# Tail additions and reciprocal products on GpSimd, q's rounding copy on VectorE, and the tail's tanh ahead of q's reads, in a fused attention and rational MLP

## The chip, the cores and the metric

The kernel runs on one core of one Trainium2 chip. The metric is the device time of one execution in microseconds; the median of three runs before is 698.41 us (698.06 to 699.09).

## What is computed

Attention with a capped score, then a two-layer MLP with a rational activation. The reference, cut to what matters:

```
scores = q @ k.T / sqrt(64)                  # 4 batches, 12 heads, 448 tokens, head size 64
scores = cap * tanh(scores / cap)            # cap = 30
attn = exp(scores - max);  attn = attn / (sum(attn) + 1e-9)
x = (attn @ v) laid out as (1792, 768)
h = x @ w_in                                 # 768 x 2048
g = (a0 + a1 h + a2 h^2 + a3 h^3) / (1 + |b0| |h| + |b1| h^2 + 1e-6)
out = g @ w_out                              # 2048 x 768
```

The weights arrive as 64-bit floats and are converted on the chip. Since cap is at most 40 the kernel takes its branch without the maximum ("bounded").

## The kernel before

**Attention.** Two heads make a pair; there are 24 pairs, p = 0 to 23. For a pair the 448 keys fall into three tiles of 128 (n = 0, 1, 2) and a tail of 64 (n = 3), in the order 0, 1, 3, 2 (`ORDER`). `scores` puts one tile's scores into one of three PSUM tiles `ps` of two banks (`slot` says which); `softmax` runs tanh there in place (L417) and `exp` writes the exponentials to SBUF (L437). A whole tile is 128 x 896 (two heads side by side); the tail is 128 x 448, with head 0 on partitions 0 to 63 and head 1 on 64 to 127. The tensor `es` of a pair collects the sum of the exponentials over the key tiles: one addition of 128 x 896 for n = 1 and one for n = 2 (L449), and for the tail two additions of 64 x 448 (L446), all on VectorE.

`pv` multiplies by v on TensorE (L494) and VectorE copies the unnormalised output to `U` (L503). After every second pair `norm` adds `es` up over the partitions on TensorE ("sums", L519, into the PSUM bank `mi`), copies the result out (L523), moves it by four small DMAs to 32 partitions, takes reciprocals (L532, L533), writes them to `dn` in HBM and reads them back broadcast over partitions (`bc`). These DMAs are on GpSimd's queue, for the last norm on SyncE's. `xout` then multiplies U by `bc` (L552, VectorE).

`prep_qk(p + 2)` is called while pair p is worked on: TensorE transposes k into bank `mi` (L335, L337) and q into the unused second bank of the tail's `ps` tile (L341). VectorE rounds k to fp32r and takes the rest (L349, L350); ScalarE scales and rounds q (L355) and VectorE takes its rest (L358). These reads of q are called before the tail's tanh.

**Conversions and splits.** During pairs 5 to 8 four weight tiles are converted (`make_w`: ScalarE L688, VectorE L690, L693, L696, then L718 and L720). x is split into a high and a low part for each of six 128-row blocks and each half of the batches: `split_x`, L563 on ScalarE and L565 on VectorE for the first half; for the second half L563 and L569 on ScalarE and a DMA on GpSimd's queue that accumulates into the low part (L570).

**MLP.** 32 units (group g of two hidden blocks, half m, block y): `stage1` (L740), `rational` (L767 to L780), `stage2` (L805). The first units of half m = 1 need the second half's splits, and so the last norms.

**Order of the work.** Every operation is recorded with an assumed cost and its reads and writes; `Plan.flush` places them by a list scheduler (priority = place in the program less `early`), for the whole program at once, and emits each engine's stream in that order. On the chip each engine, and GpSimd's queue with its DMAs, runs its stream strictly in order. So another engine, cost or write key for one operation moves other operations too.

Of the kernel before, what the change touches and what calls it, by code (L numbers as in the profile page):

```python
# [235 lines left out]
class Body:  # L236
# [83 lines left out]
    def prep_qk(self, p):  # L320
# [18 lines left out]
        def tq():  # L339
            for c in range(4):  # L340
# [6 lines left out]
        self.busy(p, 0, [])  # L347
        self.op(PE, 440, tk, self.raw_keys(p, "rk"), bk + ["turn"], early=E_TR)
# [3 lines left out]
        self.op(PE, 400, tq, self.raw_keys(p, "rq"), bq + ["turn"], early=E_TR)  # L352
        self.busy(p, 1, bq)
        c1 = self.c["c1"]
        self.op(ACT, act_ns(448, True, 1), lambda: nc.scalar.activation(S[:, 2, 0:448], pq, AF.Identity, scale=c1),  # L355
                bq, [K("qh")], early=E_PR)
        self.op(DVE, dve_ns(448, 1),
                lambda: nc.vector.scalar_tensor_tensor(QL, pq, c1, f32(S[:, 2, 0:448]), ALU.mult, ALU.subtract),  # L358
                bq + [K("qh")], [K("ql")], early=E_PR)
# [49 lines left out]
    def softmax(self, p, n):  # L409
# [6 lines left out]
        if self.bounded:  # L416
            self.op(ACT, act_ns(448 * w, True), lambda: nc.scalar.activation(ps, ps, AF.Tanh),  # L417
                    ["table"], pk)
# [12 lines left out]
    def exp(self, p, n, src, sk, e, ek):  # L431
# [115 lines left out]
    def xout(self, p):  # L547
        k, x = divmod(p, 2)
        U = self.U[p]
        i = k % len(self.BC)  # L550
        bc = f32(self.BC[i])
        self.op(DVE, dve_ns(448), lambda: self.nc.vector.tensor_tensor(U, bc[:, x], U, ALU.mult),  # L552
                [("bc", i, x, j) for j in range(2)], [("u0", p), ("u1", p)])
# [18 lines left out]
    def attention(self):  # L572
# [17 lines left out]
        for p in range(P1):  # L590
            for m, n in enumerate(ORDER):
                self.scores(p, n)
                self.softmax(p, n)
                if (p, n) == (0, 0):
# [3 lines left out]
                if m == (2 if self.bounded else 3) and p + 2 < P1:  # L598
                    self.prep_qk(p + 2)
# [275 lines left out]
    def mlp(self, rest):  # L875
# [6 lines left out]
        for t in [t for t in rest if not self.last_norm(t // 2)]:  # L882
            self.xout(t)
# [15 lines left out]
        for u, (g, m, y) in enumerate(self.units):  # L899
# [5 lines left out]
            if u == 0:  # L905
                for t in rest:
                    self.xout(t)
# [301 lines left out]
```

## Time and profile before

| | us |
|---|---|
| median of 3 runs | 698.41 |
| the profiled execution, own time | 700.66 |
| its span, first to last instruction | 698.9 |
| busy: PE / DVE / ACT / POOL | 674.0 / 565.4 / 462.5 / 101.3 |

PE is TensorE's matmuls, PEld its weight loads, DVE is VectorE, ACT ScalarE, POOL GpSimd, SP SyncE. Issuing a DMA occupies a queue, and is not counted as the engine's arithmetic. A timeline row gives start, duration, engine, line, operation, output, inputs, how many instructions were merged, and in brackets the idle time before and what ended it. A matmul counts as busy from its start to a modelled end, so that a TensorE that is "busy" may still be slower than at its best.

### The profile page before, as it was taken

To read this page: it belongs to the slowest core of one execution; us is meant where nothing else is said; L and a number is where in the kernel's file an instruction comes from. 1 tells how busy PE (TensorE), PEld (TensorE's weight loads), DVE (VectorE), ACT (ScalarE), POOL (GpSimd) and SP (SyncE) were. 2 spreads that over 40 slices of the span, in tenths; PEclk is the share of its full clock that TensorE was granted. 3 is DMA by queue.
4 is the path that set the end of the run, shared out by engine and by line. 5 is a ranking of instruction groups with operands and counts; after the bars stand their busy time and mean duration, and the time that the engine had idled before them with its cause. 6 is when DMAs were issued, how large, how long until landed. Compare 5 with 4: busy or idle time off the path is not lost.

```text
span 698.9 us, 9641 instructions
## 1 busy us (share of the span) xinstructions
PE 674.0 (96%) x3685; PEld 546.2 (78%) x3685; DVE 565.4 (81%) x706; ACT 462.5 (66%) x575; POOL 101.3 (15%) x164
## 2 busy tenths in 40 slices
PE   7999889999999899999999999999999999999986
PEld 4554445444546799999999999999999999999986
DVE  4588999999884979866998698699779869878783
ACT  5699879899996887756557448546655744754520
POOL 4012223223232200011002001101100200110000
PEclk9799999999999999999999999999999999999999
DMA  6638665554315644167119417713922751692044
GB/s 146 144 87 198 156 148 130 129 131 118 84 36 120 122 143 163 45 123 159 58 45 160 90 45 156 139 46 78 174 50 85 139 109 46 131 210 67 23 181 163
DMA packets 81912, 79.95 MB, mean 114 GB/s; under 512 B 48960, under 2 KB 69184, under 8 KB 81856
## 3 DMA queue, kind: packets, MB, share of 16 engines
q1 hardware_dynamic: 70496, 53.74, 26.4%
q0 software_dynamic: 11360, 25.50, 21.3%
q8 instruction: 31, 0.51, 0.3%
q14 instruction: 25, 0.20, 0.1%
HBM read 50.73 MB, written 25.65 MB: 109 GB/s over the span
## 4 chain that ended last, share of the span: by engine, by line
PE 76%; DVE 12%; issue 4%; ACT 3%; SPq 2%; DMA 2%; POOL 0%; DVEq 0%; POOLq 0%
PE ps L740 32%; PE ps L805 16%; PE mi L805 8%; PE pv L805 8%; PE pv L494 5%; PE ps L405 4%; DVE arena_f L449 2%; DVE arena_f L446 2%; PE ps L316 1%; ACT ps L417 1%; DVE arena_r L358 1%; DMA arena_r<-dn 1%; DVE arena_r L349 1%; SPq L283 1%; PE ps L341 1%
## 5 line engine op out<-in xcount | busy, mean ns | idle before, releaser
L740 PE MATMUL ps<-arena_r,ring 128*128 128x512 f32 (+1 forms) x1152 | 249.5, 368 | 1.9 <-DMA arena_r<-arena_f 1.7
L740 PEld LDWEIGHTS ps<-arena_r,ring 128*128 128x128 f32 x1152 | 209.2, 188 | 28.4 <-DMA arena_r<-arena_f 2.1
L805 PE MATMUL ps<-arena_r,etiles 128*128 128x384 f32 x462 | 91.1, 338 | 0.0
L417 ACT ACTIVATE ps<-ps 128x896 f32<-128x896 f32 (+1 forms) x96 | 76.4, 815 | 16.0 <-PE ps L405 11.0
L283 POOL DMA_DIRECT2D sums<-arena_f x42 | 36.5, 868 | 341.6 <-ACT arena_f L837 337.5
L771 DVE SCALAR_TENSOR_TENSOR arena_f<-arena_f,bab 128x896 f32<-128x896 f32 x32 | 36.8, 1150 | 60.2 <-ACT arena_f L768 60.2
L767 ACT ACTIVATE arena_f<-ps,b 128x896 f32<-128x896 f32 x32 | 32.3, 1011 | 77.2 <-PE ps L740 77.2
L805 PEld LDWEIGHTS ps<-arena_r,etiles 128*128 128x128 f32 x462 | 81.8, 189 | 1.6 <-ACT etiles L779 0.3
L805 PE MATMUL pv<-arena_r,etiles 128*128 128x384 f32 x231 | 77.5, 337 | 0.0
L805 PE MATMUL mi<-arena_r,etiles 128*128 128x384 f32 x231 | 77.3, 336 | 0.0
L437 ACT ACTIVATE etiles<-ps,acap 128x896 f32<-128x896 f32 x72 | 72.5, 1014 | 0.6
L779 ACT CAST etiles<-arena_f 128x896 fp32r<-128x896 f32 x32 | 30.3, 946 | 61.6 <-DVE arena_f L778 61.5
L405 PEld LDWEIGHTS ps<-arena_r 64*128 64x128 f32 x432 | 37.9, 190 | 37.1 <-ACT arena_r L355 10.5
L494 PE MATMUL pv<-etiles,ring 128*64 128x448 f32 x264 | 60.4, 566 | 0.6 <-DVE arena_f L503 0.6
L405 PE MATMUL ps<-arena_r 64*128 64x448 f32 x432 | 59.0, 396 | 0.9 <-DVE arena_r L350 0.6
L776 DVE SCALAR_TENSOR_TENSOR arena_f<-arena_f,one 128x896 f32<-128x896 f32 x32 | 36.8, 1149 | 13.8 <-ACT arena_f L774 13.8
L805 PEld LDWEIGHTS pv<-arena_r,etiles 128*128 128x128 f32 x231 | 43.7, 189 | 1.2
L805 PEld LDWEIGHTS mi<-arena_r,etiles 128*128 128x128 f32 x231 | 43.7, 189 | 0.0
L805 PE MATMUL ps<-ring,etiles 128*128 128x384 f32 x210 | 42.2, 335 | 0.8 <-DVE arena_f L834 0.8
L688 ACT ACTIVATE arena_f<-arena_f 128x768 f32<-128x768 f32 x32 | 29.2, 911 | 17.5 <-DMA arena_f<-in_moe_w_in_dram 9.2
L805 PEld LDWEIGHTS ps<-ring,etiles 128*128 128x128 f32 x210 | 36.9, 188 | 1.6 <-DVE arena_f L834 1.1
L775 DVE SCALAR_TENSOR_TENSOR arena_f<-arena_f,a,ps 128x896 f32<-128x896 f32 x32 | 36.6, 1144 | 0.6
(113 smaller groups left out, 1096.3 us busy)
## 6 DMA issues: line engine op xcount, KB each, us to landing
sums<-arena_f POOLq DMA_DIRECT2D x42, 384.0 KB, 5.9
arena_f<-in_moe_w_out_dram SPq DMA_DIRECT2D x16, 768.0 KB, 4.1
arena_f<-in_moe_w_in_dram SPq DMA_DIRECT2D x16, 768.0 KB, 8.7
out_dram<-arena_f SPq DMA_DIRECT2D x13, 384.0 KB, 2.3
ring<-in_q_dram SPq DMA_DIRECT2D x44, 112.0 KB, 3.7
arena_r<-dn POOLq DMA_DIRECT2D x22, 224.0 KB, 4.0
ring<-in_k_dram SPq DMA_DIRECT2D x33, 128.0 KB, 2.9
ring<-in_v_dram SPq DMA_DIRECT2D x11, 384.0 KB, 4.7
```

The costliest lines, as they stand in the source:

```text
L283: self.op(eng, (625 if local else 450) if eng == SP else 1050, lambda: e.dma_start(out, in_, **accum), r, w, nbytes=nbytes, **kw)
L405: m = nc.tensor.matmul(self.PS[i][:, j, 0:448], st[r], mv[r], start=y == 0, stop=y == 2)
L417: self.op(ACT, act_ns(448 * w, True), lambda: nc.scalar.activation(ps, ps, AF.Tanh), ["table"], pk)
L437: self.op(ACT, act_ns(448 * w, sk[0][0] == "ps", 1), lambda: nc.scalar.activation(e, src, AF.Exp, scale=acap), sk + ["table"], [ek])
L494: m = nc.tensor.matmul(self.PV[64 * j:64 * j + 64, 0:448], st, mv, start=c == 0, stop=c == 3)
L740: r = nc.tensor.matmul(po[:, ts], w[:, y, kc], x, start=kc == 0 and z == 0, stop=kc == KC - 1 and z == 2)
L767: self.op(ACT, act_ns(n, True, 1), lambda: T.activation(Bt, h, AF.Abs, scale=b[:, 0:1]), hk, bk)
L771: self.op(DVE, dve_ns(n, 1), lambda: stt(Bt, C, bab[:, 1:2], Bt, ALU.mult, ALU.add), ck + ["bab"], bk)
L775: self.op(DVE, dve_ns(n, 1), lambda: stt(A, A, a[:, 1:2], h, ALU.add, ALU.mult), hk, ak)
L776: self.op(DVE, dve_ns(n, 1), lambda: stt(Bt, Bt, one, C, ALU.add, ALU.mult), ck, bk)
L779: self.op(ACT, act_ns(n, False), lambda: T.copy(GH(), A), ak, K("gh", ig) + first)
L805: r = nc.tensor.matmul(po[n][:, 0:384], st, mv[:, 384 * n:384 * n + 384], start=(y == 0 and x == 0), stop=(y == self.NCH - 1 and x == 2))
```

## The change

Four edits. The tail's two additions into `es` go from VectorE to GpSimd, behind the addition of tile n = 2. `xout` goes to GpSimd, except where it is called late (for pairs 21, 22 and 23, in `mlp`). q's scaling and rounding goes from ScalarE to VectorE. And `prep_qk` is called in two parts around the tail's `softmax`: the transposes before, the reads of k and q behind; the tail's tanh declares both banks of its PSUM tile as written, so that q's reads stand behind it.

```
+def pool_ns(n):
+    return 2.0 * n + 100
...
-    def prep_qk(self, p):
+    def prep_qk(self, p, part=None):
...
+        if part != 1:
+            self.busy(p, 0, [])
+            self.op(PE, 440, tk, self.raw_keys(p, "rk"), bk + ["turn"], early=E_TR)
+        if part is None:
+            self.convert_k(S, pk, bk, K)
+        if part != 1:
+            self.op(PE, 400, tq, self.raw_keys(p, "rq"), bq + ["turn"], early=E_TR)
+            self.busy(p, 1, bq)
+        if part == 1:
+            self.convert_k(S, pk, bk, K)
+        if part == 0:
+            return
+        qh = S[:, 2, 0:448]
+        self.op(DVE, dve_ns(448, 1), lambda: nc.vector.tensor_scalar(qh, pq, c1, None, ALU.mult),
+                bq, [K("qh")], early=E_PR)
...
-        self.op(ACT, act_ns(448, True, 1), lambda: nc.scalar.activation(S[:, 2, 0:448], pq, AF.Identity, scale=c1),
-                bq, [K("qh")], early=E_PR)
...
             self.op(ACT, act_ns(448 * w, True), lambda: nc.scalar.activation(ps, ps, AF.Tanh),
-                    ["table"], pk)
+                    ["table"], [("ps", i), ("psb", i)])
...
-        if n == 0:
+        if n in (0, 3):
             return
         es, ks = self.es[p % 3], [("es", p % 3)]
-        if n == 3:
-            for j in range(2):
-                r = slice(64 * j, 64 * j + 64)
-                self.op(DVE, dve_ns(448),
-                        lambda r=r, j=j: nc.vector.tensor_tensor(es[r, j], es[r, j], e[r, 0], ALU.add), [ek], ks)
-            return
         a, ak = self.etile(p, 0) if n == 1 else (es, None)
         self.op(DVE, dve_ns(896), lambda: nc.vector.tensor_tensor(es, a, e, ALU.add), [ek] + [ak] * (n == 1), ks)
+        t, tk = self.etile(p, 3)
+        for j in range(2 if n == 2 else 0):
+            r = slice(64 * j, 64 * j + 64)
+            self.op(POOL, pool_ns(448),
+                    lambda r=r, j=j: nc.gpsimd.tensor_tensor(es[r, j], es[r, j], t[r, 0], ALU.add), [tk], ks)
...
-    def xout(self, p):
+    def xout(self, p, late=False):
...
+        eng, e = (DVE, self.nc.vector) if late else (POOL, self.nc.gpsimd)
+        self.op(eng, dve_ns(448) if late else pool_ns(448), lambda: e.tensor_tensor(U, bc[:, x], U, ALU.mult),
...
                 self.scores(p, n)
+                if self.bounded and m == 2 and p + 2 < P1:
+                    self.prep_qk(p + 2, 0)
                 self.softmax(p, n)
+                if self.bounded and m == 2 and p + 2 < P1:
+                    self.prep_qk(p + 2, 1)
```

What the scheduler makes of it, at two places. In the rows below the lines of the changed kernel are its own: L464 are the tail additions, L568 `xout`, L459 the additions of tiles 1 and 2, L365 and L368 q's copy and rest, L373 and L374 k's, L518 the copy of U, L287 DMAs. The streams of a pair are alike from pair to pair but for the conversions.

**VectorE**, an odd pair in the middle of attention, where the reciprocals of a norm fall into it. Before:

```order
L449 TENSOR_TENSOR arena_f<-etiles 128x896
L503 COPY arena_f<-pv 128x448
L446 TENSOR_TENSOR arena_f<-arena_f 64x448
L532 TENSOR_SCALAR arena_f<-arena_f,guard 32x56
L533 RECIPROCAL arena_f<-arena_f 32x56
L446 TENSOR_TENSOR arena_f<-arena_f 64x448
L349 CAST arena_r<-mi 128x512
L449 TENSOR_TENSOR arena_f<-arena_f,etiles 128x896
L350 TENSOR_TENSOR arena_r<-mi,arena_r 128x512
L358 SCALAR_TENSOR_TENSOR arena_r<-ps_130,c_61,arena_r 128x448
```

Now, the same pair:

```order
L373 CAST arena_r<-mi 128x512
L374 TENSOR_TENSOR arena_r<-mi,arena_r 128x512
L459 TENSOR_TENSOR arena_f<-etiles 128x896
L365 TENSOR_SCALAR arena_r<-ps_130,c_61 128x448
L547 TENSOR_SCALAR arena_f<-arena_f,guard 32x56
L548 RECIPROCAL arena_f<-arena_f 32x56
L368 SCALAR_TENSOR_TENSOR arena_r<-ps_130,c_61,arena_r 128x448
L518 COPY arena_f<-pv 128x448
L459 TENSOR_TENSOR arena_f<-arena_f,etiles 128x896
```

The two tail additions are gone from the stream, q's copy has come in ahead of q's rest, and the addition of tile 2, on which GpSimd's additions wait, is followed by the next pair's reads of k.

**GpSimd's queue**, from the four small DMAs of the norm of pairs 20 and 21 to the accumulations of the second half's splits. Before:

```order
L283 DMA arena_f<-arena_f 8x1x56 x4
L283 DMA arena_r<-arena_f 128x2x448
L283 DMA dn<-arena_f 32x56
L283 DMA arena_r<-arena_f 128x2x448
L283 DMA arena_r<-dn 64x896 x2
L283 DMA arena_r<-arena_f 128x2x448 x4
```

Now:

```order
L464 TENSOR_TENSOR arena_f<-arena_f 64x448
L287 DMA arena_f<-arena_f 8x1x56
L287 DMA arena_r<-dn 64x896 x2
L464 TENSOR_TENSOR arena_f<-arena_f 64x448
L287 DMA arena_f<-arena_f 8x1x56 x3
L464 TENSOR_TENSOR arena_f<-arena_f 64x448
L568 TENSOR_TENSOR arena_f<-arena_r,arena_f 128x448 x2
L464 TENSOR_TENSOR arena_f<-arena_f 64x448
L287 DMA dn<-arena_f 32x56
L287 DMA arena_r<-arena_f 128x2x448 x2
L287 DMA arena_r<-dn 64x896 x2
L568 TENSOR_TENSOR arena_f<-arena_r,arena_f 128x448
L287 DMA arena_r<-arena_f 128x2x448 x4
```

The additions of pairs 22 and 23 and the products of pairs 18 and 19 now stand between the small DMAs and the reciprocals' way to HBM (`dn`); both first accumulations stand ahead of the broadcast (the second `arena_r<-dn`; the first is that of pairs 18 and 19), and the product of pair 20 behind it.

## Rows read from the trace of the kernel before

**Rows 1.** The page: busy tenths of PE, DVE, POOL in 40 slices.
```profile
PE   7999889999999899999999999999999999999986
...
DVE  4588999999884979866998698699779869878783
...
POOL 4012223223232200011002001101100200110000
```

**Rows 2.** Busy time by stretch: window, length, PE, PEld, DVE, ACT, POOL, clock, DMA.
```profile
63.45:101.55 38.10, 33.61 (x196) 16.32 (x196) 36.56 (x56) 31.47 (x41) 9.49 (x18) 0.96 0.71 172
109.60:167.42 57.82, 53.71 (x341) 27.52 (x340) 54.56 (x80) 52.99 (x70) 16.93 (x32) 1.00 0.55 129
167.42:205.43 38.01, 37.95 (x244) 18.93 (x242) 33.62 (x52) 35.29 (x46) 11.13 (x21) 1.00 0.26 69
```

**Rows 3.** Timeline of PE: the tail's scores of pairs 3, 4 and 5.
```profile
40.91 0.89 PE L316 MATMUL ps<-arena_r 128*128 128x448 f32 x3
...
48.07 0.88 PE L316 MATMUL ps<-arena_r 128*128 128x448 f32 x3
...
56.12 0.87 PE L316 MATMUL ps<-arena_r 128*128 128x448 f32 x3
```

**Rows 4.** What PE waited for, 60 to 170 us: total, times, longest.
```profile
PE mi L335 <- DVE arena_f L523: 3.5, 4, 1.7
PE ps L316 <- ACT etiles L437: 3.4, 3, 1.7
```

**Rows 5.** Groups of instructions, 0 to 330 us, shapes apart: busy us, mean ns.
```profile
L446 DVE TENSOR_TENSOR arena_f<-arena_f 64x448 f32<-64x448 f32 x48 | 29.6, 616 | 3.4 <-ACT arena_f L437 1.7
...
L449 DVE TENSOR_TENSOR arena_f<-arena_f,etiles 128x896 f32<-128x896 f32 x24 | 26.0, 1082 | 3.6 <-ACT etiles L437 3.0
...
L358 DVE SCALAR_TENSOR_TENSOR arena_r<-ps,c,arena_r 128x448 fp32r<-128x448 f32 x23 | 15.6, 679 | 3.5 <-ACT arena_r L355 2.0 <-ACT arena_f L437 1.2 <-ACT ps L417 0.3
...
L355 ACT ACTIVATE arena_r<-ps,c 128x448 fp32r<-128x448 f32 x23 | 14.8, 642 | 4.0 <-PE ps L341 3.9
...
L552 DVE TENSOR_TENSOR arena_f<-arena_r,arena_f 128x448 f32<-128x448 f32 x24 | 14.3, 616 | 8.4 <-DMA arena_r<-dn 8.4
```

**Rows 6.** Timeline of POOL at the start: its own instructions that are no DMA.
```profile
1.51 0.29 POOL masks.py:199 TENSOR_SCALAR_AFFINE_SELECT ident<-ident 128x128 f32<-128x128 f32 x1
...
4.55 1.08 POOL L186 MEMSET ring<- 128x256 f32 x4
```

**Rows 7.** Groups of DVE, 0 to 330 us: conversion and split instructions with two SBUF inputs.
```profile
L693 DVE SCALAR_TENSOR_TENSOR arena_f<-arena_f 128x768 int32<-128x768 int32 x11 | 10.5, 953 | 0.2
...
L565 DVE TENSOR_TENSOR arena_r<-arena_f,arena_r 128x896 fp32r<-128x896 f32 x6 | 6.5, 1082 | 0.9 <-ACT arena_r L563 0.9
```

**Rows 8.** Timeline of ACT, pair 15: q's rounding copy and the tail's tanh.
```profile
145.28 0.63 ACT L355 ACTIVATE arena_r<-ps,c 128x448 fp32r<-128x448 f32 x1 [0.22 <-PE ps L341]
...
147.16 0.53 ACT L417 ACTIVATE ps<-ps 128x448 f32<-128x448 f32 x1 [0.36 <-DVE arena_r L358]
```

**Rows 9.** Timeline: pair 21's last tile-2 addition, and the sums that need it.
```profile
199.09 1.02 DVE L449 TENSOR_TENSOR arena_f<-arena_f,etiles 128x896 f32<-128x896 f32 x1
...
203.12 0.96 PE L519 MATMUL mi<-arena_f 128*32 128x448 f32 x8
```

**Rows 10.** Timeline: the hand-over from attention to the MLP.
```profile
206.30 2.00 POOL L283 DMA_DIRECT2D arena_f<-arena_f  x4 [3.79 <-DVE arena_f L523]
...
213.46 1.09 DVE L449 TENSOR_TENSOR arena_f<-arena_f,etiles 128x896 f32<-128x896 f32 x1
...
213.79 0.87 POOL L283 DMA_DIRECT2D dn<-arena_f  x1
...
218.11 1.11 POOL L283 DMA_DIRECT2D arena_r<-dn  x2
...
224.93 0.62 DVE L552 TENSOR_TENSOR arena_f<-arena_r,arena_f 128x448 f32<-128x448 f32 x1 [6.80 <-DMA arena_r<-dn]
...
234.82 1.09 PE L740 MATMUL ps<-arena_r,ring 128*128 128x512 f32 x4 [1.70 <-DMA arena_r<-arena_f]
```

More of the change, by code (lines that the diff above doesn't have):

```diff
@@ L346, in prep_qk, with convert_k @@
         K = lambda s: (name, s)
-        self.busy(p, 0, [])
-        self.op(PE, 440, tk, self.raw_keys(p, "rk"), bk + ["turn"], early=E_TR)
+        c1 = self.c["c1"]
+        if part != 1:
[13 more added lines that the diff above has]
+                bq, [K("qh")], early=E_PR)
+        self.op(DVE, dve_ns(448, 1),
+                lambda: nc.vector.scalar_tensor_tensor(QL, pq, c1, f32(qh), ALU.mult, ALU.subtract),
+                bq + [K("qh")], [K("ql")], early=E_PR)
+    def convert_k(self, S, pk, bk, K):
+        nc = self.nc
         self.op(DVE, dve_ns(512), lambda: nc.vector.tensor_copy(S[:, 1, :], pk), bk, [K("kh")], early=E_PR)
@@ L351, in prep_qk @@
                 bk + [K("kh")], [K("kl")], early=E_PR)
-        self.op(PE, 400, tq, self.raw_keys(p, "rq"), bq + ["turn"], early=E_TR)
-        self.busy(p, 1, bq)
-        c1 = self.c["c1"]
-        self.op(ACT, act_ns(448, True, 1), lambda: nc.scalar.activation(S[:, 2, 0:448], pq, AF.Identity, scale=c1),
-                bq, [K("qh")], early=E_PR)
-        self.op(DVE, dve_ns(448, 1),
-                lambda: nc.vector.scalar_tensor_tensor(QL, pq, c1, f32(S[:, 2, 0:448]), ALU.mult, ALU.subtract),
-                bq + [K("qh")], [K("ql")], early=E_PR)
     def busy(self, p, n, r):
@@ L551, in xout @@
         bc = f32(self.BC[i])
-        self.op(DVE, dve_ns(448), lambda: self.nc.vector.tensor_tensor(U, bc[:, x], U, ALU.mult),
+        eng, e = (DVE, self.nc.vector) if late else (POOL, self.nc.gpsimd)
+        self.op(eng, dve_ns(448) if late else pool_ns(448), lambda: e.tensor_tensor(U, bc[:, x], U, ALU.mult),
                 [("bc", i, x, j) for j in range(2)], [("u0", p), ("u1", p)])
@@ L597, in attention @@
                     self.load_v(1, [(self.qset(1)[0], "ql")])
-                if m == (2 if self.bounded else 3) and p + 2 < P1:
+                if not self.bounded and m == 3 and p + 2 < P1:
                     self.prep_qk(p + 2)
@@ L882, in mlp @@
         for t in [t for t in rest if not self.last_norm(t // 2)]:
-            self.xout(t)
+            self.xout(t, True)
         rest = [t for t in rest if self.last_norm(t // 2)]
@@ L906, in mlp @@
                 for t in rest:
-                    self.xout(t)
+                    self.xout(t, True)
             if u == 1:
```

## The prediction, made before the changed kernel ran

> **What bounds the kernel now.** I read the page's slices first. TensorE is at nine tenths or more in nearly all of them, VectorE at eight and nine in the first fifteen, which are attention, and GpSimd at two or less from slice three on [rows 1]. So the end is set by TensorE, and by VectorE where TensorE falls short. The MLP behind 240 us is TensorE's alone and the change does not touch it; what is to be won lies in attention.
>
> TensorE's own pace there comes from the timeline of its tail scores, once per pair: 7.16 us from pair 3 to 4, 8.05 us from 4 to 5, which holds a norm's sums [rows 3]. That is 15.21 us for two pairs. Against this I set three stretches that begin and end at tail scores [rows 2]:
>
> - pairs 6 to 10, with the weight conversions: 38.10 us, where four pairs at TensorE's pace take 30.42. 7.7 us over; VectorE is busy for 36.56, so it sets the pace.
> - pairs 11 to 18, with the first splits: 57.82 us, where four times 7.16 and three times 8.05 make 52.79. 5.0 us over; VectorE 54.56 busy, ScalarE 52.99.
> - pairs 18 to 23: 38.01 us, TensorE 37.95 busy. Nothing to win.
>
> So at most 12.7 us lie in attention. How VectorE holds TensorE there: k's transposes wait for VectorE's copy out of the bank `mi` (3.5 us), the tail's scores for the exponentials of the tile before (3.4) [rows 4]. The latter are late because the tail's tanh, next on ScalarE, starts only when VectorE has taken q's rest: q's copy began at 145.28, tanh at 147.16 after a wait on L358 [rows 8].
>
> **The change, part by part.** *VectorE.* Per pair two tail additions of 616 ns and one product of 616 ns go [rows 5]: 1.85 us. q's copy comes. No row shows this form; from PSUM with a scalar it is nearest to q's rest at 679 ns, and at the low end stands the 616 ns of an addition of 448 columns [rows 5]. I take 0.65. VectorE is relieved of 1.2 us per pair: 4.8 us in the conversion stretch, 8.4 in the split stretch.
>
> *ScalarE* loses q's copy, 642 ns per pair [rows 5], and its wait behind L358. It is no bound afterwards: 52.99 less 4.5 in 52.79. q's copy must now wait for tanh, but both banks are wanted again only after two stretches of `pv`, so I cost this at nothing; what covers it is TensorE's work between, and without that it would cost about tanh's length, half a microsecond, per pair.
>
> *GpSimd* gets three operations per pair whose price the trace does not show. A memset of 256 columns took 1.08/4 = 0.27 us, 1.05 ns a column for one write; the select of 128 columns, one read and one write, 0.29 us, 2.27 ns a column [rows 6]. For 448 columns the select's rate gives 1.02 us; with a second read at the memset's rate 1.49. Below stands VectorE's 0.62. I take 1.1, near the row that reads and writes. That is 3.3 us per pair beside 16.93/7 = 2.4 us of DMA issues [rows 2]: 5.7 of 7.6, so the queue keeps up. The Trainium skill (GPSIMD Engine Reference, section 3.1) gives 4497 ns for an addition of 2048 columns, by which 448 would be an estimate of 0.98 us; the sum, with it in the hold-up and the hand-over below, would be some 1.3 us less.
>
> *Hold-up between the two engines.* Nothing in the trace of before runs arithmetic on GpSimd beside VectorE, so this is bounded. The low end is nothing. The high end is that an operation of GpSimd that meets a VectorE operation with two SBUF inputs makes VectorE lose the whole 1.1 us. Such operations fill half of VectorE's time in the conversion stretch (per pair two additions of 1.08, two conversions of 0.95 and the shorter third, some 4.6 of 9.1 us) and four tenths in the split stretch [rows 5, 7]: at most 1.65 and 1.3 us per pair. I take half, 0.8 and 0.65, because either engine may be the one that waits, and GpSimd's waiting costs nothing while its queue has room.
>
> So the conversion stretch gains 4 x (1.2 - 0.8) = 1.6 us; VectorE stays the bound there. In the split stretch VectorE comes to 54.56 - 8.4 + 7 x 0.65 = 50.7, with the 3.3 us that it idled before 54.0: a gain of 3.8 of the 5.0.
>
> *The hand-over.* Here GpSimd's queue is on the path. Before, the small DMAs of the norm of pairs 20 and 21 ran from 206.30 to 208.30, the reciprocals went out at 213.79, the broadcast at 218.11, pair 20's product ran at 224.93, and TensorE waited 1.70 us for the accumulation behind it, to 234.82 [rows 10]. Now the queue, as the order in the section on the change shows, has pair 23's first addition in front of the reciprocals' way out. That needs VectorE's addition, which ended at 214.55 [rows 10]; then come four operations of 1.1 us, so `dn` is issued near 219.0. Two accumulations follow (1.2 us each) before the broadcast, near 221.9 instead of 218.1, and the product takes 1.1 instead of 0.62. All that hangs on it is some 4 us later. TensorE has the first tiles of the second layer to do ahead of those splits, about 2 us, and ScalarE, free of splits that now run earlier, may bring pair 23's exponentials 1 us forward. Bounds: nothing, if the cover holds, and 5 us. I take a loss of 2.5.
>
> **Sum:** -1.6 - 3.8 + 2.5 = -2.9 us. The profiled execution took 700.66 us, with a span of 698.9 and 1.8 around it; it would take 697.8. It is 2.25 us above the median of 698.41; for the median I forecast **695.5 us**.
>
> **The rivals.**
>
> *No hold-up* (chance 0.22): the engines run side by side. Then the conversions gain 4.8, the splits their whole 5.0, less 2.5: -7.3, 691.1 us. For it: ScalarE and TensorE read the same memory all along, and VectorE's additions come out alike, 616 ns in both forms [rows 5]. Against: those are other engines.
>
> *GpSimd and VectorE lock each other out* (0.25): every meeting costs VectorE the whole operation. The place is the conversion stretch: 1.65 us lost per pair for 1.2 won, so four pairs lose 1.8; the splits come to 54.56 - 8.4 + 9.1 + 3.3 = 58.6, 0.7 slower; and the stretched queue makes the hand-over 3.5 us later. +6.0, 704.4 us. It decides from a loss of 1.2 us per pair on; with the hand-over, slower begins at about 0.9. For it: VectorE is full there. Against: behind the addition that releases GpSimd stand k's copy and rest, 1.4 us with a PSUM input. The Trainium skill (SBUF — State Buffer, section Who interferes with whom) says so as a rule: a VectorE instruction with two SBUF inputs and a GpSimd instruction that reads SBUF exclude each other for the whole instruction, and whichever starts first makes the other wait. By that rule either may lose, and the time lies between the likeliest case and 704.4. No run so far shows it.
>
> *The sums wait for GpSimd* (0.13): pair 21's last VectorE addition ended at 200.11 and the sums began at 203.12 [rows 9], 3.0 us. Two additions of 1.1 and three hand-offs leave 0.5. If DMA issues stand ahead in the queue, of 0.5 us each (2.00 for four [rows 10]), TensorE waits some 0.3 us in each of 11 norms: -5.4 + 3.0 + 2.5, about 698.5, no change. It also covers the case that the saving of VectorE does not reach TensorE.
>
> **How the numbers follow.** The likeliest case has 0.40; its own range is from 692 to 699, the bounds of the copy, GpSimd's price and the hand-over. About 0.2% (1.4 us) is what a measurement of this kernel can tell from no change. Faster: 0.35 of the likeliest, all 0.22 of the first rival, 0.03 of the third: 0.60. Within: 0.04 of the likeliest, 0.02 of the second and 0.09 of the third: 0.15. Slower: the rest of all, 0.25. The range leaves out the ends of both extreme rivals: 690 to 703.5.
>
> **What would show it.** In the profile after, the tail scores of pairs 6 to 10 should take 36 to 37 us and those of 11 to 18 53 to 55; tanh should no longer wait for q's rest; GpSimd's additions should take 1.0 to 1.3 us. VectorE's additions of tiles 1 and 2, 1.08 us before, show hold-up if their mean grows by more than 0.1; the sums waiting for GpSimd would show the third rival. Between 205 and 245 us TensorE should idle 3 to 5 us instead of 2, behind the accumulation of the third block. I am wrong if attention's two stretches do not shorten, or if the hand-over loses more than 5 us.

## The result, and the profile after

The changed kernel takes **705.36 us** (704.10 to 705.91, four runs) beside 698.35 for the kernel before on the same chip: a ratio of **1.008**, 95% interval [1.006, 1.0099]. It is slower; the forecast was 695.5 us, with 703.5 as the upper end of its range. The quotient of the two medians alone would be 1.010 (7.0 us); the tables below use the ratio on record, 1.008 (5.6 us). The profiled execution took 705.91 us with a span of 704.0 us; that of before had 698.9. The spans differ by 5.1 us only, mostly because the profiled execution of before lies 2.3 us above its median and that of the changed kernel 0.5.

The page of the changed kernel, busy time and slices (to compare with [rows 1]):

```profile
PE 676.5 (96%) x3685; PEld 544.4 (77%) x3685; DVE 560.3 (80%) x661; ACT 450.9 (64%) x551; POOL 186.9 (27%) x233
...
PE   6899899999999799999999999999999999999986
...
DVE  4579988999873868877898798789879869779783
...
POOL 3346767877875300011002001100200200110000
```

VectorE has 45 instructions less (69 gone to GpSimd, 24 come for q) and yet only 5.1 us less of busy time, where 69 times 0.616 less 24 times 0.657 would be 27. GpSimd has 85.6 us more.

The same three stretches as [rows 2] (pairs 6 to 10, 11 to 18, 18 to 23), with the columns of that group:

```profile
64.20:100.61 36.41, 33.42 (x197) 17.10 (x197) 34.77 (x47) 29.48 (x37) 23.85 (x30) 0.95 0.65 158
109.51:167.81 58.30, 54.93 (x342) 27.47 (x340) 53.56 (x66) 50.01 (x63) 43.26 (x54) 1.00 0.58 129
167.81:206.78 38.97, 38.68 (x243) 19.10 (x241) 31.02 (x41) 32.99 (x42) 29.39 (x36) 1.00 0.22 58
```

The conversions got 1.7 us shorter, the splits 0.5 longer, the last pairs 1.0 longer. From here on I measure the **22 intervals** (start of the tail's scores of pair 1 to that of pair 23; TensorE alone would need some 166.5 us at the pace of [rows 3], the last pairs being shorter as they prepare no other) and the **rest** (from there to the end of the span). Before: 181.4 and 493.5 us. After: 182.3 and 497.2. So in these two executions attention won nothing and the hand-over lost 3.7.

Groups of instructions, 0 to 330 us (busy us, mean ns, idle before; to compare with [rows 5, 7]). First the kernel before, the addition of tile 1 and the guard (a small operation ahead of the reciprocals, 32x56); then the changed kernel:

```profile
L449 DVE TENSOR_TENSOR arena_f<-etiles 128x896 f32<-128x896 f32 x24 | 26.1, 1086 | 4.6 <-ACT etiles L437 4.6
...
L532 DVE TENSOR_SCALAR arena_f<-arena_f,guard 32x56 f32<-32x56 f32 x12 | 2.8, 234 | 0.1
```

```profile
L464 POOL TENSOR_TENSOR arena_f<-arena_f 64x448 f32<-64x448 f32 x48 | 60.2, 1254 | 50.1 <-DVE arena_f L459 44.7 <-DVE bab L909 2.6 <-PE ps L320 1.1
L459 DVE TENSOR_TENSOR arena_f<-etiles 128x896 f32<-128x896 f32 x24 | 32.9, 1372 | 7.0 <-ACT etiles L453 6.7 <-POOL arena_f L464 0.3
L459 DVE TENSOR_TENSOR arena_f<-arena_f,etiles 128x896 f32<-128x896 f32 x24 | 29.7, 1236 | 3.3 <-ACT etiles L453 3.3
...
L365 DVE TENSOR_SCALAR arena_r<-ps,c 128x448 fp32r<-128x448 f32 x23 | 15.1, 657 | 4.4 <-ACT arena_f L453 4.1 <-PE ps L345 0.2
L713 DVE SCALAR_TENSOR_TENSOR arena_f<-arena_f 128x768 int32<-128x768 int32 x11 | 11.6, 1053 | 0.1
...
L547 DVE TENSOR_SCALAR arena_f<-arena_f,guard 32x56 f32<-32x56 f32 x12 | 8.2, 687 | 4.7 <-DMA arena_f<-arena_f 4.7
L581 DVE TENSOR_TENSOR arena_r<-arena_f,arena_r 128x896 fp32r<-128x896 f32 x6 | 7.4, 1237 | 0.0
```

VectorE's operations that read two tensors from SBUF got longer, 1.09 to 1.37, 1.08 to 1.24, 0.95 to 1.05, 1.08 to 1.24, and the guard, which reads one, from 0.23 to 0.69. q's rest (L368), which has one input in PSUM, did not: 679 ns before, 670 now; nor did the reciprocals behind the guard, 491 ns in both. Two cases, in the timeline of VectorE and then of GpSimd in the same kernel:

```profile
64.83 2.47 DVE L459 TENSOR_TENSOR arena_f<-arena_f,etiles 128x896 f32<-128x896 f32 x1
...
119.63 2.29 DVE L547 TENSOR_SCALAR arena_f<-arena_f,guard 32x56 f32<-32x56 f32 x1
```

```profile
65.19 1.16 POOL L568 TENSOR_TENSOR arena_f<-arena_r,arena_f 128x448 f32<-128x448 f32 x1
...
119.63 1.15 POOL L568 TENSOR_TENSOR arena_f<-arena_r,arena_f 128x448 f32<-128x448 f32 x1
120.73 1.14 POOL L464 TENSOR_TENSOR arena_f<-arena_f 64x448 f32<-64x448 f32 x1
```

The addition, 1.09 alone, took 2.47 us around a product of 1.16. The guard, 0.23 alone, took 2.29 us: exactly the two GpSimd operations of 1.15 and 1.14 that ran in that time.

What TensorE waited for, 60 to 250 us (total, times, longest; to compare with [rows 4]):

```profile
PE mi L534 <- POOL arena_f L464: 3.4, 2, 2.0
PE ps L760 <- DVE arena_f L795: 3.3, 2, 2.3
PE ps L421 <- DVE arena_r L368: 2.2, 4, 0.7
PE mi L339 <- DVE arena_f L538: 1.3, 3, 0.8
```

The old waits of [rows 4] are down from 6.9 us to 1.5 (L339, and 0.2 of L320 for the exponentials). The sums (L534) now wait for GpSimd, 2.0 us once in the conversions and 1.4 once in the splits; the 3.3 us of L760 lie in the hand-over. There (GpSimd's timeline, to compare with [rows 10]) the reciprocals go out at 219.26 instead of 213.79, the broadcast at 222.78 instead of 218.11, and pair 20's product runs at 230.50 instead of 224.93:

```profile
218.15 1.16 POOL L464 TENSOR_TENSOR arena_f<-arena_f 64x448 f32<-64x448 f32 x1
219.26 0.52 POOL L287 DMA_DIRECT2D dn<-arena_f  x1
...
222.78 1.13 POOL L287 DMA_DIRECT2D arena_r<-dn  x2 [0.45 <-DMA dn<-arena_f]
...
230.50 1.14 POOL L568 TENSOR_TENSOR arena_f<-arena_r,arena_f 128x448 f32<-128x448 f32 x1 [6.59 <-DMA arena_r<-dn]
```

But TensorE does not wait for the accumulation behind that product any more, as it did for 1.70 us before [rows 10]. It waits for VectorE's L795, an operation of the MLP's rational function. The last sums of the kernel before; then, in the changed kernel, the last sums, TensorE's wait, and VectorE:

```profile
216.47 0.96 PE L519 MATMUL mi<-arena_f 128*32 128x448 f32 x8
```

```profile
220.56 0.96 PE L534 MATMUL mi<-arena_f 128*32 128x448 f32 x8
...
233.89 3.85 PE L760 MATMUL ps<-arena_r,ring 128*128 128x512 f32 x12 [2.26 <-DVE arena_f L795]
```

```profile
230.85 0.84 DVE L547 TENSOR_SCALAR arena_f<-arena_f,guard 32x56 f32<-32x56 f32 x1 [2.54 <-DMA arena_f<-arena_f]
...
232.62 1.12 DVE L795 SCALAR_TENSOR_TENSOR arena_f<-arena_f,a,ps 128x896 f32<-128x896 f32 x1
```

L795 stands in VectorE's stream behind the guard of the last norm, which waits for that norm's small DMAs, and these follow the last sums. The last sums start 13.8 us after the last tail scores (206.78), where it was 11.0 (205.43); ahead of them in time is GpSimd's addition for pair 23, which ends at 219.31.

### The profile page after: what moved, and what is told of

It is laid out like the page before. It is cut to its first block, busy times and chain, and to the rows that moved or that the text cites. A ratio compares the mean times of both kernels' runs of the same rounds, so it can differ in the third digit from the quotient of the medians.

```text
span 704.0 us, 9702 instructions
## 1 busy us (share of the span) xinstructions
PE 676.5 (96%) x3685; PEld 544.4 (77%) x3685; DVE 560.3 (80%) x661; ACT 450.9 (64%) x551; POOL 186.9 (27%) x233
## 4 chain that ended last, share of the span: by engine, by line
PE 74%; DVE 7%; DMA 6%; ACT 4%; issue 4%; POOL 2%; SPq 1%; POOLq 0%; DVEq 0%; ACTq 0%
PE ps L760 29%; PE ps L825 14%; PE mi L825 7%; PE pv L825 7%; PE pv L509 7%; PE ps L421 4%; DMA arena_f<-arena_f 2%; DMA arena_f<-in_moe_w_in_dram 1%; ACT etiles L453 1%; PE ps L320 1%; POOL arena_f L464 1%; DMA arena_r<-dn 1%; ACT ps L433 1%; DVE arena_f L459 1%; SPq L287 1%
## 5 line engine op out<-in xcount | busy, mean ns | idle before, releaser
L760 PE MATMUL ps<-arena_r,ring 128*128 128x512 f32 (+1 forms) x1152 | 251.4, 369 | 3.5 <-DVE arena_f L795 3.3
L760 PEld LDWEIGHTS ps<-arena_r,ring 128*128 128x128 f32 x1152 | 209.6, 188 | 32.0 <-ACT arena_r L579 2.6
L287 POOL DMA_DIRECT2D sums<-arena_f x42 | 36.5, 870 | 343.3 <-ACT arena_f L857 342.0
L464 POOL TENSOR_TENSOR arena_f<-arena_f 64x448 f32<-64x448 f32 x48 | 60.2, 1254 | 50.1 <-DVE arena_f L459 44.7
L453 ACT ACTIVATE etiles<-ps,acap 128x896 f32<-128x896 f32 x72 | 70.3, 1012 | 0.7
L421 PEld LDWEIGHTS ps<-arena_r 64*128 64x128 f32 x432 | 37.9, 191 | 41.3 <-ACT ps L433 14.2
L421 PE MATMUL ps<-arena_r 64*128 64x448 f32 x432 | 60.8, 400 | 3.8 <-DVE arena_r L368 2.7
L459 DVE TENSOR_TENSOR arena_f<-etiles 128x896 f32<-128x896 f32 x24 | 32.9, 1372 | 7.0 <-ACT etiles L453 6.7
```

The source lines that it names most:

```text
L287: self.op(eng, (625 if local else 450) if eng == SP else 1050, lambda: e.dma_start(out, in_, **accum), r, w, nbytes=nbytes, **kw)
L421: m = nc.tensor.matmul(self.PS[i][:, j, 0:448], st[r], mv[r], start=y == 0, stop=y == 2)
L453: self.op(ACT, act_ns(448 * w, sk[0][0] == "ps", 1), lambda: nc.scalar.activation(e, src, AF.Exp, scale=acap), sk + ["table"], [ek])
L464: lambda r=r, j=j: nc.gpsimd.tensor_tensor(es[r, j], es[r, j], t[r, 0], ALU.add), [tk], ks)
L760: r = nc.tensor.matmul(po[:, ts], w[:, y, kc], x, start=kc == 0 and z == 0, stop=kc == KC - 1 and z == 2)
```

## The experiments

All ratios are to the kernel before, on the same chip; 0.001 is 0.7 us. Intervals and rest come from each kernel's one profiled execution. Executions of a kernel spread over 1 to 6 us (the kernel before from 696.75 to 702.30 on one chip), and the profiled one can lie at an end (e4's took 694.5, its median is 695.39), so a difference of intervals or rest below some 2 us is not shown by them.

| run | tail additions | products | q's copy | time us | ratio [95%] | 22 intervals | rest |
|---|---|---|---|---|---|---|---|
| before (tanh behind) | VectorE | VectorE | ScalarE | 698.35 | 1 | 181.4 | 493.5 |
| after | GpSimd | GpSimd | VectorE | 705.36 | 1.008 [1.006, 1.0099] | 182.3 | 497.2 |
| e1 | VectorE | GpSimd | VectorE | 707.66 | 1.0115 [1.0074, 1.0157] | 186.5 | 495.9 |
| e2 | GpSimd | VectorE | VectorE | 701.67 | 1.0024 [0.9999, 1.005] | 182.5 | 495.1 |
| e3 | VectorE | VectorE | VectorE | 701.34 | 1.0031 [1.0009, 1.0054] | 184.5 | 492.1 |
| e4 | VectorE | VectorE | ScalarE | **695.39** | **0.9942** [0.9921, 0.9963] | 175.6 | 493.1 |
| e5 | GpSimd | GpSimd | ScalarE | 704.6 | 1.0074 [1.0052, 1.0096] | 182.1 | 496.5 |
| e6 | GpSimd | VectorE | ScalarE | 699.7 | 1.0003 [0.9981, 1.0026] | 175.1 | 497.1 |

**Parts undone and parts alone (e1 to e6).** All have the tail's tanh ahead of q's reads. The edits, each of the changed kernel: additions back (e1, e3, e4), products back (e2, e3, e4, e6), q's copy back (e4, e5, e6).

```
+        if n == 3:
+            for j in range(2):
+                self.op(DVE, dve_ns(448),
+                        lambda r=r, j=j: nc.vector.tensor_tensor(es[r, j], es[r, j], e[r, 0], ALU.add), [ek], ks)
+            return
...
-    def xout(self, p, late=False):
+    def xout(self, p, late=True):
...
-        self.op(DVE, dve_ns(448, 1), lambda: nc.vector.tensor_scalar(qh, pq, c1, None, ALU.mult),
+        self.op(ACT, act_ns(448, True, 1), lambda: nc.scalar.activation(qh, pq, AF.Identity, scale=c1),
```

> Only the tail additions go back to VectorE, at their old place ahead of tile 2's; products stay on GpSimd, q's copy on VectorE, tanh ahead. Theory A (GpSimd's operations and VectorE's two-input operations hold each other up, and the sums wait for GpSimd's additions): without the sums' wait and with a third of GpSimd's operations, attention from pair 1 to 23 takes about 180 us instead of 182.3, additions of tiles 1 and 2 average 1.12 to 1.18 us instead of 1.24 and 1.37; 700 to 703 us. Rival B (hold-up costs nothing, the sums' wait is all): 697 to 699. Rival C (q's copy on VectorE or the order around tanh is at fault): no better than 704.

> Only the products go back to VectorE; tail additions stay on GpSimd. Theory A: GpSimd's queue is shorter, so the sums wait less, and the hand-over loses its extra wait, but VectorE has 0.62 us per pair more; 700 to 703 us, additions of tiles 1 and 2 at 1.15 to 1.25 us. Rival B (the sums' wait is all): the wait stays in most norms, 703 to 706. Rival C: no better than 704.

> Additions and products both back on VectorE; q's copy stays on VectorE and tanh ahead. No arithmetic on GpSimd. Theory A: no hold-up, no wait of the sums; VectorE has 0.65 us per pair more than before the change: 697 to 701 us, additions of tiles 1 and 2 back at 1.08 us. Rival C (q's copy or the order around tanh): 703 to 707.

> The kernel before with nothing but the tail's tanh ahead of q's reads. Theory A: ScalarE's wait behind q's rest goes, VectorE as before: 694 to 698 us, at or below before. Rival C (the order around tanh is at fault): above 700.

> The changed kernel with q's rounding copy back on ScalarE; additions and products stay on GpSimd. Theory D (q's copy on VectorE is the dearest part: it lies in VectorE's chain tanh, copy, rest that frees the PSUM bank; without arithmetic on GpSimd it cost 5.9 us): 698 to 701 us, attention from pair 1 to 23 at most 179 us. Theory A (hold-up and the sums' wait alone): 703 to 706 us, attention as long as the changed kernel's 182.3.

> Tail additions on GpSimd and tanh ahead; products on VectorE, q's copy on ScalarE. Compared with the tanh-only kernel at 695.4. Theory D: VectorE has 1.2 us per pair less and some hold-up back, and attention there is already within 2 us of TensorE's pace: 693 to 697 us, no more than 2 us either way. Theory A: hold-up and the sums' wait eat more than the relief: 698 to 702 us.

Read as a chain, the parts cost: tanh ahead -4.0 us (e4), then the additions on GpSimd +4.3 (e6), then the products on GpSimd +5.0 (e5), then q's copy on VectorE +0.4 (after; within the error). The places differ: the additions lose in the rest (493.1 to 497.1), while attention takes 175.1 us beside 175.6, though VectorE's addition of tile 1 has 1285 ns there; the products lose in attention (175.1 to 182.1). Without arithmetic on GpSimd the last part alone costs 6 us (e3 against e4): there VectorE is busy for 56.91 of the 57.62 us of the splits. Tanh ahead is the one part that pays. e2 against the changed kernel gives the products alone in another company: back on VectorE they win 3.9 us. In e1 the products on GpSimd alone lengthen the additions of tile 1 to 1250 ns and those of the tail to 680. e1 missed the expected 700 to 703 upwards; VectorE is busy in it for 55.41 of the 57.05 us of the splits. e2, e4 and e5 came as their theory A had them, e3 0.3 us above it; e6's time did too, but not by a loss in attention.

How tanh ahead pays is seen in ScalarE's waits, 24 to 210 us; the kernel before, then e4:

```profile
ACT ps L417 <- PE ps L405: 7.8, 12, 2.2
ACT arena_f L437 <- DVE arena_r L358: 3.4, 4, 1.1
ACT ps L417 <- DVE arena_r L358: 2.9, 6, 1.2
```

```profile
ACT ps L433 <- PE ps L421: 10.9, 16, 1.6
```

The 6.3 us in which ScalarE waited for VectorE's rest of q are gone, and nearly all that is left is waiting for TensorE. But the chain is not clean: each of these kernels also has an order of its own.

**The same order, GpSimd only writes (e7, e10, e16).** These keep the changed kernel's order on every engine. Each addition is replaced by two (e7) or three (e10) clears; e16 also replaces each product by three. The tail is left out of the sums, and in e16 the products of GpSimd are left out.

```
-    lambda r=r, j=j: nc.gpsimd.tensor_tensor(es[r, j], es[r, j], t[r, 0], ALU.add), [tk], ks)
+    lambda r=r, j=j: [nc.gpsimd.memset(es[r, j], 1.0) for _ in range(3)], [tk], ks)
...
-    ... lambda: e.tensor_tensor(U, bc[:, x], U, ALU.mult),
+    ... lambda: e.tensor_tensor(U, bc[:, x], U, ALU.mult) if late else [e.memset(U, 1.0) for _ in range(3)],
```

> The changed kernel with each tail addition on GpSimd replaced by two memsets of the same 64 x 448: GpSimd writes there and reads nothing, and the tail is left out of the sums. If GpSimd's reads are what VectorE's two-input operations collide with: additions of tile 1 fall from 1.37 to at most 1.2 us (the products still read), and 700 to 703 us. If any work on GpSimd holds VectorE up: they stay at 1.3 or more, and the time within 2 us of the changed kernel's.

> Each tail addition on GpSimd is replaced by three clears of 64 x 448 values, some 1.4 us a tile and so longer than the addition, with nothing read; the tail is left out of the sums. Theory A, GpSimd's reads lengthen VectorE's two-operand work: additions of n==1 at 1.10-1.17 us, intervals 176-178.5 us, time 698-701 us. Theory B, the length of GpSimd's occupation decides (it releases the sums and the products late): n==1 additions 1.10-1.40, intervals 181 us or more, time 704 us or more.

> The changed kernel in its own order, with each tail addition and each of GpSimd's products replaced by three clears of the same size (1.42 us, longer than the 1.25 us that they took), so that GpSimd reads no SBUF; the tail is left out of the sums and the products are left out. Theory A, the reads cost: additions of n==1 and n==2 at 1.08-1.12 us, intervals 175-178 us, time 696-699.5 us. Theory B, the length of GpSimd's chain costs: intervals 178-181, time 701-705 us.

e7: 698.83 us, 0.9978 [0.996, 0.9996], below the 700 to 703 expected; intervals 177.0, rest 496.4. e10: 702.31, 1.0028 [1.001, 1.0047]; 178.4 and 498.6. e16: 698.66, 0.9975 [0.9957, 0.9992]; 176.1 and 497.9. Groups of e10, then of e16:

```profile
L459 DVE TENSOR_TENSOR arena_f<-arena_f,etiles 128x896 f32<-128x896 f32 x24 | 30.2, 1259 | 3.1 <-ACT etiles L453 3.1
L568 POOL TENSOR_TENSOR arena_f<-arena_r,arena_f 128x448 f32<-128x448 f32 x21 | 27.3, 1300 | 15.7 <-DMA arena_r<-dn 13.7 <-DMA ring<-in_k_dram 1.3 <-issue 0.3
L459 DVE TENSOR_TENSOR arena_f<-etiles 128x896 f32<-128x896 f32 x24 | 26.1, 1086 | 8.6 <-ACT etiles L453 7.9 <-POOL arena_f L464 0.7
```

```profile
L464 POOL MEMSET arena_f<- 64x448 f32 x144 | 68.3, 474 | 45.7 <-DVE arena_f L459 37.2 <-DVE bab L909 1.8
L568 POOL MEMSET arena_f<- 128x448 f32 x63 | 29.8, 476 | 2.8
L459 DVE TENSOR_TENSOR arena_f<-etiles 128x896 f32<-128x896 f32 x24 | 26.1, 1086 | 9.4 <-ACT etiles L453 9.0 <-POOL arena_f L464 0.3
L459 DVE TENSOR_TENSOR arena_f<-arena_f,etiles 128x896 f32<-128x896 f32 x24 | 26.0, 1082 | 3.2 <-ACT etiles L453 3.2
...
L547 DVE TENSOR_SCALAR arena_f<-arena_f,guard 32x56 f32<-32x56 f32 x12 | 4.4, 364 | 5.8 <-DMA arena_f<-arena_f 5.8
```

This is the clearest reading of the study. GpSimd is busier than in the changed kernel (197.8 us against 186.9), but where it reads nothing VectorE's additions are back at 1086 and 1082 ns. In e10, where only the products still read, the addition of tile 2, which they meet, stays at 1259, and that of tile 1, which the tail's additions met, is at 1086. The guard is the exception: at 364 ns it is held up by clears too, though less than by reads (687). From e16 to e10 the products' reads cost 3.7 us, from e10 to the changed kernel the additions' reads 3.6: **7.3 us for reading**, by the 95% intervals of the two ratios within some 2 us either way; 6.2 us of it lie in the 22 intervals (176.1 to 182.3). GpSimd's length costs too: the third clear (e7 to e10) 3.5 us, so e10 misses the 698 to 701 that reads alone would have given; nor does it reach the length theory's 704.

The stretches of e16, in the same columns as above, show the rate:

```profile
62.96:99.07 36.11, 33.42 (x199) 16.67 (x197) 32.16 (x46) 29.50 (x37) 26.14 (x53) 0.95 0.74 181
107.12:161.50 54.38, 54.26 (x342) 28.01 (x340) 46.17 (x65) 49.91 (x63) 45.97 (x96) 1.00 0.66 143
```

VectorE does the same work, but for what the ends of the stretches cut off, in 32.16 instead of 34.77 us and in 46.17 instead of 53.56: by reads it is held up by 2.6/4 = **0.65 us per pair** beside the conversions and 7.4/7 = **1.06** beside the splits. In the splits TensorE is then busy for 54.26 of 54.38 us. The conversions, though, are only 0.3 us shorter than in the changed kernel, with VectorE idle for 4 us: TensorE waits there for GpSimd's additions, 2.0 us in the changed kernel and as long in e16 (60 to 250 us):

```profile
PE mi L534 <- POOL arena_f L464: 2.1, 1, 2.1
```

**The same order, the work on VectorE (e15).** The plan of the changed kernel is kept, and the additions and products are issued on VectorE.

```
-    lambda r=r, j=j: nc.gpsimd.tensor_tensor(es[r, j], es[r, j], t[r, 0], ALU.add), [tk], ks)
+    lambda r=r, j=j: nc.vector.tensor_tensor(es[r, j], es[r, j], t[r, 0], ALU.add), [tk], ks)
...
-    eng, e = (DVE, self.nc.vector) if late else (POOL, self.nc.gpsimd)
+    eng, e = (DVE if late else POOL), self.nc.vector
```

> The changed kernel with its plan kept, so that TensorE's and ScalarE's order is the same, but the tail's additions and the products are issued on VectorE, at the place in the order that they have on GpSimd. VectorE then has 1.85 us more per pair. Theory A, the hold-up and the wait for a slow engine cost more than the relief: VectorE's additions at 1.08-1.10 us, time 697-702 us, so 3 us or more below the changed kernel. Theory B, the order of the change costs, whoever does the work: 704-708 us.

709.03 us, 1.011 [1.0073, 1.0147]; intervals 187.5, rest 495.6; additions at 1084 and 1083 ns. So in this order the work was not better off on VectorE, against the hold-up theory's figure, and the time is above the order theory's 708 too. Beside e3, which does the same work on the same engines in an order planned for it (1.0031), an order planned for GpSimd costs 5.5 us, 3.5 of them in the rest. That holds where VectorE does the work at GpSimd's places; what the order costs the changed kernel itself is not shown by it. That gives a second chain, each step behind e3 with one thing changed: before, e3 +2.2 us (tanh ahead, q's copy on VectorE), e15 +5.5 (the plan that counts on GpSimd), e16 -9.4 (work off VectorE, GpSimd only writes), after +7.3 (GpSimd reads). The sum is +5.6, that is 1.008.

**Additions that nothing waits for (e13, e14).** To e4, whose order stays the same instruction by instruction on TensorE, and on VectorE but for one pair, GpSimd gets work per pair that only writes a spare strip: seven additions that read the tail's tile, or seventeen clears.

```
+        if n == 2 and p < 21:
+            (t, tk), z = self.etile(p, 3), self.Z
+            self.op(POOL, 0, lambda: [nc.gpsimd.tensor_tensor(z, t[:, 0, 0:176], t[:, 0, 176:352], ALU.add) for _ in range(7)], [tk], ["z"])
```

> The kernel with only tanh ahead (395.. all arithmetic as before on VectorE, 695.4 us, 22 intervals of 176.1 us), and besides, per pair up to pair 20, seven additions of 128 x 176 on GpSimd that nothing waits for: they read the pair's tail tile and write a spare strip. Theory A, GpSimd's reads hold up VectorE's work with two SBUF operands: VectorE's additions of n==1 or n==2 rise from 1.08 to 1.15-1.40 us in the mean, intervals 180-184 us, time 700-704 us. Theory B, the cost of the change lies in who waits for GpSimd and in the order, not in a hold-up: additions stay at 1.08-1.10, intervals 176-177.5, time 695-697 us.

> The same with seventeen clears of 128 x 176 per pair in place of the seven additions, about as long and with nothing read. Theory A: additions stay at 1.08-1.10 us, intervals 176-177.5, time 695-697 us, so 4 us or more below the kernel with the seven additions. Theory B: the two kernels agree within 1.5 us.

e13: 741.19 us, 1.057 [1.0539, 1.06]; e14: 707.37, 1.0098 [1.0076, 1.0119]. Groups of e13, then of e14:

```profile
L468 POOL TENSOR_TENSOR arena_f<-arena_f 128x176 f32<-128x176 f32 x147 | 124.7, 849 | 38.1 <-ACT arena_f L453 28.0
L462 DVE TENSOR_TENSOR arena_f<-arena_f 64x448 f32<-64x448 f32 x48 | 35.4, 737 | 1.5 <-ACT arena_f L453 0.7
L465 DVE TENSOR_TENSOR arena_f<-arena_f,etiles 128x896 f32<-128x896 f32 x24 | 29.4, 1223 | 1.2 <-ACT etiles L453 0.5
L465 DVE TENSOR_TENSOR arena_f<-etiles 128x896 f32<-128x896 f32 x24 | 27.7, 1153 | 2.2 <-ACT etiles L453 2.0
```

```profile
L468 POOL MEMSET arena_f<- 128x176 f32 x357 | 88.1, 247 | 19.4
L462 DVE TENSOR_TENSOR arena_f<-arena_f 64x448 f32<-64x448 f32 x48 | 29.4, 612 | 1.5 <-ACT arena_f L453 0.7
L465 DVE TENSOR_TENSOR arena_f<-etiles 128x896 f32<-128x896 f32 x24 | 26.0, 1085 | 2.4 <-ACT etiles L453 2.2
L465 DVE TENSOR_TENSOR arena_f<-arena_f,etiles 128x896 f32<-128x896 f32 x24 | 26.0, 1082 | 1.5 <-ACT etiles L453 0.8
```

That reads lengthen VectorE's operations with two SBUF inputs and writes don't is confirmed, with nobody waiting for GpSimd's result. Both times miss what I expected, and their size is not that of the hold-up: VectorE's busy time grew by 15 us from e4 to e13 (563.9 to 578.9), the time by 44. Seven additions took 5.9 us per pair, more than I had meant, and with 2.4 us of DMA issues the queue was full. VectorE's waits, 24 to 210 us, of e13 and then of e14, show what that does:

```profile
DVE arena_f L572 <- DMA arena_r<-dn: 23.3, 5, 6.2
```

```profile
DVE arena_f L572 <- DMA arena_r<-dn: 10.4, 5, 3.3
```

In e4 this wait, of the products for the broadcast, was 0.8 us in all. The norm's DMAs stand behind GpSimd's work, VectorE waits for them in order, and q's rest behind it comes late for TensorE (waits of 8.8 us in e14, 2.0 in e4). Four us per pair of clears that nobody waits for cost e14 11 us over e4, and this wait is the one that grew most (0.8 to 10.4 us). In e13 the clock adds to it: in pairs 11 to 18 TensorE is idle for 15.0 of 73.1 us and is granted 0.91 of its full clock, where e4 has 1.00, and its busy time is 58.1 us instead of 53.5.

**Order and hand-over (e8, e9, e11, e12).** e8: products of pairs 18 to 20 on VectorE. e9: the tail's sums one score tile later. e11: GpSimd's price in the plan 1.265 instead of 0.996 us. e12: e6 with the tail additions of pairs 21 to 23 on VectorE.

```
-                        self.xout(t)
+                        self.xout(t, t >= 18)
...
-                    if m == 3 and p % 2 == 0:
-                        norm(p // 2 - 1)
+                if self.bounded and m == 0 and p % 2 and p > 1:
+                    norm((p - 3) // 2)
...
-    return 2.0 * n + 100
+    return 2.6 * n + 100
...
+            eng, e2 = (POOL, nc.gpsimd) if p < 21 else (DVE, nc.vector)
```

> The changed kernel with the products of pairs 18 to 20 on VectorE as well: nothing but tail additions stands ahead of the last reciprocals in GpSimd's queue. If the later hand-over is GpSimd's queue: from the last tail scores to the end 493.5 to 495 us instead of 497.2, 701 to 703.5 us. If it is something else (the splits' order on ScalarE): 497 again, 704 to 706.

> The changed kernel, with the tail's sums and everything behind them of two pairs called one score tile later in the odd pair. Theory A, TensorE stands where it reaches the tail's sums before GpSimd has finished the additions (waits of 1.4 to 2.0 us on the trace of the change): the waits on GpSimd's additions fall under 1 us in all, the 22 intervals from pair 1 to pair 23 shrink from 182.3 to 179-180.5 us, the time falls to 702-704 us. Theory B, reading by GpSimd lengthens VectorE's operations and the sums are only where it shows: n==1 additions stay at 1.33-1.40 us, the intervals stay at 181.5-183, the time is 704.5-706.5 us.

> The changed kernel with GpSimd's price in the plan raised from 0.996 to 1.265 us for 448 columns, which is nearer to what its additions take here. Theory A, the plan counts on an engine that is faster than the real one, so the order sends TensorE to the sums too early: waits on GpSimd shrink, time 700-703 us. Theory B, the order is not what costs: intervals 181.5-183.5, time 704-707 us.

> The kernel with tanh ahead and the tail's additions on GpSimd (products on VectorE, q's copy on ScalarE), but the tail's additions of pairs 21 to 23 back on VectorE. Theory A, the late additions of the last pairs on GpSimd delay the last sums and reciprocals and so the output projection: the stretch behind the last tail scores falls from 497.1 to 492.5-494 us, time 695-697 us. Theory B, something else lengthens that stretch (the order behind pair 18, the wide loads): it stays at 496-498 us, time 699-701 us.

e8: 705.24, 1.0073 [1.0046, 1.0099], rest 497.8: those products are not what delays the hand-over. e9: 705.81, 1.0081 [1.0054, 1.0107]; TensorE's wait for the tail's additions falls from 3.4 to 1.2 us and the time does not: its waits for VectorE (L339, L421) grow from 3.5 to 5.7. e12: 699.01, 0.9984 [0.9956, 1.0011]; the rest falls from e6's 497.1 to 494.0 as expected, the intervals grow from 175.1 to 179.2 with the new order, most of the gain is gone, and the time misses the expected 695 to 697. The last sums start 11.3 us after the last tail scores, where it is 12.5 in e6 and 11.0 in e4. So the tail additions of the last pairs, standing late in the order, are most of what the hand-over loses (3.0 of 3.9 us from e4 to e6), as far as one can tell with another order in all of it. e11 missed both theories: **720.77 us**, 1.0288 [1.0247, 1.033], intervals 198.5. TensorE waits in it for GpSimd's additions for 10.3 us (60 to 250 us), where it was 3.4 in the changed kernel. A price nearer to the chip made a worse order, by 15 us. Which places of that order do it I did not follow; in pairs 6 to 10 TensorE is granted 0.88 of its full clock (0.95 in the changed kernel) and is busy for 37.2 us instead of 33.4, which is part of it.

## Why the prediction was wrong

1. *What bounds attention, and tanh.* Right for the splits: VectorE held TensorE through q's rest and the exponentials. Tanh ahead wins 4.0 us by itself (e4). The prediction had it as a shift of waits with no term of its own. In the conversions the bound was misread in part: of the 7.7 us that were put down to VectorE, 3.2 lie in TensorE's own busy time, 33.61 us [rows 2] instead of 30.42, at a granted clock of 0.96.
2. *GpSimd's price.* Right: taken at 1.1 us, 1.13 to 1.16 where it runs alone, 1.25 in the mean. The Trainium skill (GPSIMD Engine Reference, section 3.1) led to an estimate of 0.98; the measurement is above it.
3. *q's copy.* Right in size: 0.65 taken, 0.657 measured.
4. *The relief.* Right in size for VectorE's busy time: without GpSimd's reads the splits take 46.17 us of it (e16), and 54.56 - 8.4 makes 46.2. In time it was worth far less. The rival without hold-up had 7.3 us to win; e16, where GpSimd reads nothing, wins 1.7 (0.9975): the splits win 3.4, the conversions 2.0, and the rest loses 4.5.
5. *The hold-up.* **The step that failed.** It was taken at half its bound, 0.8 us per pair in the conversions and 0.65 in the splits, "because either engine may be the one that waits". Measured: 0.65 in the conversions, but 1.06 in the splits, nearer to the upper bound of 1.3. So the splits lost 0.5 us where 3.8 were to be won. In the same order without GpSimd's reads this stretch takes 54.38 us instead of 58.30 (e16): 3.9 of the 4.3 us by which the forecast missed it come with the reads. With 1.06 the prediction's own formula gives 54.56 - 8.4 + 7.4 + 3.3 = 56.9 us; the 1.4 us that are left are as long as TensorE's wait for the sums there, but that this is their cause is not shown (e9 shortens that wait and is no faster). The estimate also left out the guard (0.23 to 0.69 us).
6. *The sums' wait.* It was a rival of its own, at 0.13, and it came together with the hold-up: 3.4 us. The 1.4 us in the splits are gone without the reads (e16); the 2.0 in the conversions are there without them too. Nothing in the prediction let two cases add up.
7. *The hand-over.* `dn` was forecast near 219.0 and came at 219.26, the broadcast near 221.9 and came at 222.78. The loss was 3.7, not 2.5. But the path was another than the one forecast: TensorE waits for VectorE's rational, behind the last norm, and no longer for the accumulation. With fewer products in the queue (e8) the rest stays at 497.8, with the last tail additions back on VectorE (e12) it is 494.0, and without any reads it is 497.9 (e16).
8. *The order.* No term at all. The plan made for GpSimd costs 5.5 us where VectorE does the work in it (e3 to e15), and a changed price in the plan 15 us (e11). What it costs in the changed kernel itself stays open.

Against the profiled span of before (-2.9 forecast, +5.1 measured), the splits are off by 4.3, the hand-over by 1.2, and the first and last pairs, taken at nothing, by some 2; the start of pair 1 half a microsecond.

The conversions came as forecast (-1.6, measured -1.7), and that is luck. VectorE was to stay the bound there; but in e16 it is busy for 2.6 us less and the stretch is only 0.3 us shorter, and e4, with no relief at all, takes 34.5 us for it (with one conversion of 0.95 us fewer in it).

The lock-out rival's 704.4 lies near the result, with a chance of 0.25, in the splits by its mechanism: +0.7 (measured +0.5). Its hand-over, +3.5 (+3.7), agrees by luck, for it came from GpSimd's stretched operations, and the rest is as long without the reads (497.9). Its loss in the conversions did not come. The Trainium skill (SBUF — State Buffer, section Who interferes with whom) says that a VectorE instruction with two SBUF inputs contends with a GpSimd instruction that reads SBUF and not with one that only writes it. The traces agree, 1372 ns with reads and 1086 without; I should have given that rule more weight than "either may wait".

The version that beats both kernels is e4, tanh ahead alone: 695.39 us, 0.9942 [0.9921, 0.9963].

## What to carry to other kernels

Work that reads SBUF on GpSimd is not free beside a full VectorE: for each GpSimd operation, count up to its whole length against a VectorE operation with two SBUF inputs that it meets, and only the rest as relief. A stretch that takes the forecast time does not yet bear out the reason given for it: look at what the engines waited for in it. Before arithmetic goes on a queue that also issues DMAs, look for who waits for those DMAs. And where a planner orders the work, an edit has two effects, the work and the order; keep the order while the work changes, and measure each alone.

## What was not expected of the hardware

A 32x56 operation of VectorE with one tensor input and one value per partition beside it (the guard) took 2.29 us instead of 0.23 while two GpSimd operations ran, so operations with two tensor inputs are not the only ones held up. This one is held up by writes as well: in e16, where GpSimd only clears, it took 0.30 to 0.60 us in eight of its twelve runs, each time beside a clear. GpSimd's additions cost little by the column: seven of 128x176 took 5.12 us at the least (e13), 0.73 us each, while 64x448 and 128x448 both took some 1.14.
